# Two open units of VectorE's exponentials with alternating passes, and a normalisation on PE that is held until its input is made

## The chip, the cores and the metric

The kernel runs on one core of one Trainium2 chip. The metric is device time of one execution in microseconds, lower is better. Before the change three runs took 967.95, 971.15 and 971.46 us; the median is 971.15 us.

The engines named here: PE (TensorE, the matmuls; PEld are its weight loads), DVE (VectorE), ACT (ScalarE), POOL (GpSimd) and SP (SyncE, which issues the DMAs).

## The reference

One transformer block on x of shape 1 x 2048 x 640, bf16: layernorm, attention with 32 heads of 20 dimensions over all 2048 positions (no mask), output projection and residual; then layernorm, a gated bilinear layer (gate times up, 1728 wide, no nonlinearity), down projection and residual.

```python
def _A_ref(x, wqkv, wo):
    ...
    q, k, v = qkv[0], qkv[1], qkv[2]
    scores = jnp.einsum("bhqd,bhkd->bhqk", q, k) * (Dh ** -0.5)
    p = _softmax(scores, axis=-1)
    o = jnp.einsum("bhqk,bhkd->bhqd", p, v)
    return (lambda x, *d: x.transpose(*d))(o, 0, 2, 1, 3).reshape(B, S, D) @ wo
def _B_ref(x, w_gate, w_up, w_down):
    g = jnp.einsum("bsd,df->bsf", x, w_gate)
    u = jnp.einsum("bsd,df->bsf", x, w_up)
    h = g * u
    return jnp.einsum("bsf,fd->bsd", h, w_down)
x = A_x
h = x + _A_ref(_layernorm(x, axis=-1), A_wqkv, A_wo)
h2 = h + _B_ref(_layernorm(h, axis=-1), B_w_gate, B_w_up, B_w_down)
```

## The kernel before

The 2048 queries are four blocks of 512 (`QB`), the 32 heads eight groups of four (`HPG`), the 2048 keys sixteen tiles of 128. A *unit* is the 128 x 512 block of scores of one head, one key tile and one query block; 2048 such units are needed. They are laid out one after another into score tiles of 1536 columns (`EW`), three units each, so that there are 683 tiles. Two score tiles fit in PSUM (`scp`), and the exponential of a tile goes to one of six `E` buffers (`ep`).

The units are ordered by *segments* (`segs`): one pass over the keys for one head group and one query block, 64 units or some 21 tiles. Pass 0 does query block 0 (its first four groups by chunks of four key tiles while the keys are still being made), passes 1 and 2 the next two blocks. Of the last block two groups go as pass 3 and the rest as two half blocks of 256 queries, passes A and B.

The whole order of instructions is worked out in Python while the kernel is built: a planner keeps the times at which it thinks that each engine will be free (`at["pe"]`, `at["dve"]`, `at["exp"]` for ScalarE, `at["slot"]` for the score tiles, `at["mi"]` for the one PSUM bank of the side jobs). The main loop takes one tile per round:

- `emit_S` (L440) issues the tile's score matmuls (L450), asks `x_takes` (L474) whether VectorE shall take the last 512 columns, and issues ScalarE's exponential of the rest (L463).
- `emit_AV` (L588) issues up to eight matmuls of the weighted sums (L619) from `av_q`, the queue of finished exponentials; when a segment is complete VectorE copies the sums out of the single `acc` bank into `asb` (L630).
- `run_job` (L429) issues a piece of other matmul work while the next tile's place is not yet free: projections, and behind the attention of each query block the output projection (`out`), the gated layer (`glu`) and its down projection (`y`) of that block. Jobs are generators that yield their PE cost; `step` (L365) takes from `urgent`, then `waiting`, then `jobs`. Where nothing fits, two matmuls keep the PE clock up (`keep_warm`, L427).
- `spare` (L412) issues pending VectorE work where the planner sees VectorE free: layernorm pieces (`aux`) first, then passes of VectorE's exponentials.

**VectorE's exponential** (`emit_x`, L480) is five instructions on 128 x 512: scale and shift out of PSUM (`xv`, L488), bits of the mantissa (`xm`, L498), two polynomial passes (`xt`, L499 and L500), and the sum that is read as bf16 (`xe`, L493). Each reads what the one before it wrote. The first is issued with its tile; the other four go into `x_pieces`, one queue in order, which `step_x` (L513) empties. `x_takes` allows a unit only in segments of kind "only" of passes 0 to 2 (or later, when no job is left), at least three tiles (`X_LEAST`) before the segment's last tile, with fewer than three pieces pending, with VectorE's planned time not over PE's by 200 ns (`TOL`), and with fewer than six (`X_OUT`) units between opening and use. `need_x` (L521) issues all that is pending of a segment before its last weighted sums, and `put_x` (L504) appends finished units to the end of their segment in `av_q`.

**The normalisation** of a segment normally goes over DMAs: sums to DRAM and back into rows, reciprocal, broadcast, multiplication on GpSimd (`norm`, L525). For the three segments of `FAST` (the last group of pass 2, the last of pass A, the last but one of pass B) it is a job on PE instead (`job_norm`, L574): f32 matmuls turn the sums into columns (L559), VectorE takes the reciprocal and spreads it (L563, L565), f32 matmuls turn it back (L571), and VectorE multiplies (L582). It is put into `urgent` as soon as the copy to `asb` has been issued, and `step` takes it at once.

The planner's own numbers: a unit costs VectorE 690 ns for the first pass and 480, 700, 700 and 700 for the others; an exponential costs ScalarE 50 ns and 5/6 ns a column; a switch on PE 110 ns (`SWITCH`), a semaphore 150 ns (`LAT`).

## Time and profile before

| | |
|---|---|
| median of three runs | 971.15 us |
| profiled execution | 968.8 us |
| its span | 966.9 us |
| mean PE clock granted | 0.976 |
| first `xv` (L488) to the last | 141.45 to 684.12 us |
| `xv` instructions | 102 |
| pass L498, mean | 438 ns |
| pass L499, mean | 695 ns |
| passes L500 and L493, mean each | 726 ns |
| keep-warm matmuls (L427) | 189, 61.6 us |
| ScalarE's wait for score tiles (L450), whole span | 22.0 us in 29 waits |
| ScalarE's wait for weighted sums (L619), whole span | 3.5 us in 3 waits |
| PE's wait for ScalarE before score tiles | 55.6 us in 128 waits |

In the lines of a profile, L12 is line 12 of the kernel; `E<-sc` means that E is written from sc; the figures behind the bar are busy microseconds, mean nanoseconds of one, and the time that the engine stood idle just before such instructions, with what ended it. In timeline lines the first two figures are start and duration in microseconds, and the bracket holds the idle time before the instruction and its releaser. Durations on VectorE can overlap: the next instruction may start before the record of the one before it ends. The span leaves out some two microseconds that lie around it in the run's time.

### The profile page before, as it was taken

The page shows a single profiled execution, that of the slowest core. Times are in us where ns is not written, and L with a number is a line of the kernel's source. Part 1 is how long each engine was busy: PE and PEld are TensorE (multiplying, and loading weights), DVE is VectorE, ACT ScalarE, POOL GpSimd, SP SyncE. Part 2 cuts the span into 40 slices and gives each one's busy share as a digit, 9 for nine tenths or more (in the row PEclk, how much of TensorE's full clock was granted, in tenths as well). Part 3 has the DMA queues.
Part 4 walks back from the last instruction along what each step waited for, and adds up shares of the span by engine and source line. Part 5 has one row for each costly group of instructions (what it writes and reads, how often), then busy time and mean ns, then how long its engine had stood idle before and what let it go on. Part 6 is the DMA issues. An engine that isn't in the chain of part 4 may idle for free.

```text
span 966.9 us, 18074 instructions
## 1 busy us (share of the span) xinstructions
PE 837.9 (87%) x7176; PEld 328.5 (34%) x7257; DVE 606.3 (63%) x1224; ACT 899.6 (93%) x719; POOL 61.6 (6%) x155
## 2 busy tenths in 40 slices
PE   7778889888887898998898999988888899888897
PEld 5233333222232222331233223322332334444465
DVE  7664348888778778888878887878462231143243
ACT  6879999999999999999999999999799999899951
POOL 3120011000000000000000000000000000000000
PEclk9999999999999899997999999999799999899999
DMA  6000010010050131014021230103202001102310
GB/s 184 28 1 1 1 26 24 20 39 13 20 178 2 39 85 43 20 43 177 7 68 33 67 87 13 34 20 104 65 3 67 19 8 27 55 19 63 75 42 17
DMA packets 67819, 44.46 MB, mean 46 GB/s; under 512 B 18504, under 2 KB 63404, under 8 KB 67728
## 3 DMA queue, kind: packets, MB, share of 16 engines
q1 hardware_dynamic: 67728, 43.23, 16.0%
q8 instruction: 59, 0.97, 0.4%
q14 instruction: 32, 0.26, 0.1%
HBM read 35.91 MB, written 7.30 MB: 45 GB/s over the span
## 4 chain that ended last, share of the span: by engine, by line
ACT 40%; PE 35%; issue 14%; DVE 9%; DMA 1%; POOL 0%; SPq 0%; ACTq 0%; DVEq 0%; POOLq 0%
ACT E L463 40%; PE sc L450 9%; PE acc L619 6%; PE mi L278 4%; PE mi L900 3%; PE mi L955 3%; PE mi L834 2%; PE f L900 2%; PE mi L427 1%; PE mi L292 1%; PE f L955 1%; DVE kT L285 1%; DVE st L182 1%; PE mi L918 1%; DVE u L247 1%
## 5 line engine op out<-in xcount | busy, mean ns | idle before, releaser
L463 ACT ACTIVATE E<-sc 128x1536 bf16<-128x1536 f32 (+1 forms) x683 | 882.3, 1460 | 27.1 <-PE sc L450 22.0
L450 PE MATMUL sc<-qa,kT 32*128 32x512 bf16 x1536 | 204.6, 390 | 54.2 <-ACT E L463 43.4
L450 PEld LDWEIGHTS <-kT 32*128 32x128 bf16 x2432 | 84.5, 91 | 293.2 <-issue 254.5
L619 PE MATMUL acc<-E,vx 128*32 128x512 bf16 (+1 forms) x2330 | 169.5, 357 | 0.5 <-ACT E L463 0.5
L488 DVE TENSOR_SCALAR xv<-sc 128x512 f32<-128x512 f32 x102 | 70.3, 689 | 38.9 <-PE sc L450 38.2
L278 PE MATMUL mi<-lnT,wp 128*128 128x512 bf16 x284 | 79.5, 380 | 14.0 <-DVE qa L285 6.6
L450 PE MATMUL sc<-qb,kT 32*128 32x256 bf16 (+1 forms) x896 | 69.6, 294 | 14.7 <-ACT E L463 12.3
L549 POOL TENSOR_TENSOR on<-asb,bc 128x512 bf16<-128x512 f32 (+1 forms) x30 | 36.0, 1198 | 718.1 <-DMA bc<-scr 468.7
L500 DVE SCALAR_TENSOR_TENSOR xt<-xt,xm 128x512 f32<-128x512 f32 x102 | 74.0, 726 | 2.3
L493 DVE SCALAR_TENSOR_TENSOR xe<-xt,xv 128x512 int16<-128x512 f32 x102 | 74.0, 726 | 1.3
L499 DVE SCALAR_TENSOR_TENSOR xt<-xm 128x512 f32<-128x512 int32 x102 | 70.9, 695 | 2.2
L619 PEld LDWEIGHTS <-vx 128*32 128x32 bf16 x2432 | 44.4, 96 | 67.4 <-issue 67.2
L955 PE MATMUL mi<-wd,hh 128*128 128x320 bf16 x378 | 66.0, 301 | 0.3 <-DVE xr L959 0.3
L427 PE MATMUL mi<-kT,ident 128*128 128x512 bf16 x189 | 61.6, 397 | 4.0 <-DVE on L582 1.8
L900 PE MATMUL mi<-ln2T,wu 128*128 128x512 bf16 (+1 forms) x158 | 46.0, 387 | 6.0 <-DVE hh L908 5.4
L955 PEld LDWEIGHTS <-hh 128*128 128x128 bf16 x448 | 38.1, 97 | 38.1 <-issue 26.6
L247 DVE CAST u<-mi 128x512 bf16<-128x512 f32 (+1 forms) x42 | 28.9, 688 | 34.9 <-PE mi L900 33.3
L908 DVE TENSOR_TENSOR hh<-mi,u 128x512 bf16<-128x512 f32 (+1 forms) x42 | 28.8, 686 | 33.9 <-PE mi L900 31.3
L900 PE MATMUL mi<-ln2T,wg 128*128 128x512 bf16 (+1 forms) x160 | 44.7, 381 | 5.9 <-DVE u L247 5.3
L498 DVE TENSOR_SCALAR xm<-xv 128x512 int32<-128x512 int32 x102 | 44.7, 438 | 0.5
L278 PEld LDWEIGHTS <-wp 128*128 128x128 bf16 x310 | 25.9, 97 | 55.6 <-issue 39.5
L834 PE MATMUL mi<-wo,on 128*128 128x320 bf16 x224 | 38.4, 303 | 1.5 <-DVE xr L838 1.3
(150 smaller groups left out, 611.3 us busy)
## 6 DMA issues: line engine op xcount, KB each, us to landing
bc<-scr SPq DMA_DIRECT2D x100, 64.0 KB
wu<-in_B_w_up_dram SPq DMA_DIRECT2D x20, 320.0 KB
wg<-in_B_w_gate_dram SPq DMA_DIRECT2D x20, 320.0 KB
qsp<-qa SPq DMA_DIRECT2D x8, 384.0 KB
xr<-in_A_x_dram SPq DMA_DIRECT2D x16, 160.0 KB
out_dram<-xr SPq DMA_DIRECT2D x14, 160.0 KB
wd<-in_B_w_down_dram SPq DMA_DIRECT2D x13, 160.0 KB
xs<-in_A_x_dram SPq DMA_DIRECT2D x3, 640.0 KB
```

The lines of the kernel that those rows point to most:

```text
L278: nc.tensor.matmul(ps[:], lhsT=wslice(m, g, c), rhs=lnT[:, c, ch * QB:(ch + 1) * QB], start=(c == 0), stop=(c == KT - 1))
L427: nc.tensor.matmul(ps[:], lhsT=ident[:], rhs=kT[0][:, 0:BANK], start=True, stop=True)
L450: nc.tensor.matmul(sc[:, o:o + w], lhsT=kT[g][SLOT * j:SLOT * (j + 1), kt * P:(kt + 1) * P], rhs=q_of(g, b, c0, w)[SLOT * j:SLOT * (j + 1) ...
L463: exps = nc.scalar.activation(e[:, 0:n_act], sc[:, 0:n_act], ACT.Exp, bias=EXP_BIAS, scale=SM_SCALE)
L488: took = nc.vector.tensor_scalar(v[:], ps, X_SCALE, X_BASE, ALU.mult, ALU.max)
L493: nc.vector.scalar_tensor_tensor(e[:], t[:], X_C, v[:], ALU.add, ALU.add)
L499: (700, lambda: nc.vector.scalar_tensor_tensor(t[:], m[:], X_A, m[:], ALU.mult, ALU.mult)),
L500: (700, lambda: nc.vector.scalar_tensor_tensor(t[:], t[:], X_B, m[:], ALU.add, ALU.mult)),
L619: nc.tensor.matmul(acc["t"][SLOT * j:SLOT * (j + 1), 0:w], lhsT=vx[kt][:, VS * h:VS * h + SLOT], rhs=e, start=(acc["n"][j] == 0), stop=(ac ...
L834: nc.tensor.matmul(ps[:, 0:HALF], lhsT=on[g][:, t * P:(t + 1) * P], rhs=wo[g][:, cs], start=(g == 0), stop=(g == NG - 1))
L900: nc.tensor.matmul(ps[0:M, 0:n], lhsT=st["w", fp][k][:, c, f2 * P:f2 * P + M], rhs=st["ln2T"][:, c, c0:c0 + n], start=(c == 0), stop=(c == ...
L955: nc.tensor.matmul(ps[:, 0:HALF], lhsT=st["hh"][f][0:K, t * P:(t + 1) * P], rhs=late["Wd"][f][0:K, cs], start=(f == 0), stop=(f == 2 * FP ...
```

## The change

- **Chains.** `x_pieces` becomes `x_chains`, one queue of passes for each open unit, and a unit may be opened while one other is open (`len(x_chains) < 2`, where it was fewer than three pending pieces). `next_x` picks the first chain other than the one whose pass was issued last on VectorE; a chain's last pass is not taken ahead of an older chain. Any other VectorE work in between clears that memory (`x_prev`). `step_x` charges 90 ns less (`X_DEP`) for a pass that does not follow its own chain.
- **Limits.** With more than two passes pending a unit must lie six tiles ahead of its segment's last tile, otherwise three as before. `X_OUT` is five instead of six, and live units are a queue that is emptied in order, so that a unit counts until it and all older ones are used. `xm` and `xt` have two buffers.
- **Normalisation on PE.** `opens` holds the planned time at which `asb` is ready, and `first` keeps the job in `urgent` until then, unless there is nothing else to do. `job_norm` now tells the planner its PE and VectorE costs and is two pieces instead of three; `sums_to_rows` is split so that its matmuls come from `sums_on_pe`.
- **Weighted sums.** `emit_AV` looks at the oldest exponential in the queue, where it looked at the first, and goes on although the `acc` bank isn't planned free when the oldest is `E_BUFS` (six, as before) rounds old; the main loop calls it a second time in a round when the oldest is five rounds old or more.

```diff
--- before.py
+++ after.py
@@ -55,7 +55,8 @@
 EXP_NS, EXP_END, EXP_COL = 50, 166, 5 / 6
 S_NS, S_EXP, SWITCH, LAT = 323, 500, 110, 150
 TOL, LEAST, MARGIN = 200, 430, 100
-X_LEAST, X_OUT = 3, 6
+X_LEAST, X_OUT, X_DEP = 3, 5, 90
+E_BUFS = 6
 SHIFT = 1184.0
 LOG2E = 1.4426950408889634
 X_UNIT = 128.0
@@ -93,7 +94,7 @@
     qkp = pool("qkp")
     vp = pool("vp")
     onp = pool("onp")
-    ep = pool("ep", 6)
+    ep = pool("ep", E_BUFS)
     nrm = pool("nrm", 2)
     xp = pool("xp")
     small = pool("small", 2)
@@ -229,6 +230,7 @@
     def dve(ns):
         ready = at["pe"] + LAT
         spare(ready)
+        x_prev["chain"] = None
         at["dve"] = max(at["dve"], ready) + ns
 
     def apply1(t, m32, r, k, eng=None):
@@ -326,11 +328,12 @@
         tiles.append((cur_t, pos))
 
     last_tile = {s: i for i, (us, _) in enumerate(tiles) for s, *_ in us}
-    x_pieces = deque()
+    x_chains = deque()
+    x_prev = {"chain": None}
     x_left = {}
     x_put = []
-    x_live = {"units": 0}
-    x_last = set()
+    x_live = deque()
+    x_used = set()
 
     av_q = deque()
     acc = {"seg": None, "t": None, "from": 0, "left": 0}
@@ -339,6 +342,7 @@
     jobs = deque()
     urgent = deque()
     waiting = deque()
+    opens = {}
     aux = deque()
     events = []
     cur = {"key": None, "gen": None, "fresh": True}
@@ -362,11 +366,14 @@
             events.remove(ev)
             ev[1]()
 
+    def first():
+        return urgent and (opens.get(urgent[0][0], 0) < at["pe"] + SWITCH or not (waiting or jobs or cur["gen"]))
+
     def step():
-        if cur["fresh"] and (urgent or waiting):
+        if cur["fresh"] and (first() or waiting):
             if cur["gen"] is not None:
                 jobs.appendleft((cur["key"], cur["gen"]))
-            cur["key"], cur["gen"] = (urgent or waiting).popleft()
+            cur["key"], cur["gen"] = (urgent if first() else waiting).popleft()
         c = advance()
         if c == WAIT:
             waiting.append((cur["key"], cur["gen"]))
@@ -404,13 +411,14 @@
         while aux:
             try:
                 at["dve"] += next(aux[0]) or 200
+                x_prev["chain"] = None
                 return True
             except StopIteration:
                 aux.popleft()
         return False
 
     def spare(until):
-        while at["dve"] + (x_pieces[0][0] if x_pieces and not aux else 600) <= until + TOL:
+        while at["dve"] + (next_x()[0][0] if x_chains and not aux else 600) <= until + TOL:
             if not step_aux() and not step_x():
                 break
 
@@ -419,7 +427,7 @@
             if not step_aux():
                 raise RuntimeError(f"nothing makes {key}")
 
-    COST = {"T": 300, "v": 680}
+    COST = {"T": 300, "v": 680, "nf": 780}
 
     def keep_warm():
         ps = bank()
@@ -428,8 +436,9 @@
 
     def run_job(until):
         if cur["fresh"]:
-            key = urgent[0][0] if urgent else cur["key"] if cur["gen"] is not None else jobs[0][0] if jobs else None
-            if not waiting and (key is None or max(at["pe"], at["mi"]) + SWITCH + COST.get(key[0], LEAST) > until):
+            key = urgent[0][0] if first() else cur["key"] if cur["gen"] is not None else jobs[0][0] if jobs else None
+            begin = max(at["pe"], at["mi"], opens.get(key, 0))
+            if not waiting and (key is None or begin + SWITCH + COST.get(key[0], LEAST) > until):
                 return key is not None
         begun = at["pe"]
         while at["pe"] + 216 <= until + 60:
@@ -474,31 +483,31 @@
     def x_takes(i):
         us, n = tiles[i]
         s = us[-1][0]
-        return (n == EW and segs[s][4] == "only" and (PASS[segs[s][0]][0] < LAST_B or not jobs and not cur["gen"]) and last_tile[s] - i >= X_LEAST and len({u[0] for u in us}) == 1
-                and len(x_pieces) < 3 and at["dve"] < at["pe"] + TOL and x_live["units"] < X_OUT)
+        return (n == EW and segs[s][4] == "only" and (PASS[segs[s][0]][0] < LAST_B or not jobs and not cur["gen"]) and last_tile[s] - i >= X_LEAST + (3 if sum(map(len, x_chains)) > 2 else 0) and len({u[0] for u in us}) == 1
+                and len(x_chains) < 2 and at["dve"] < at["pe"] + TOL and len(x_live) < X_OUT)
 
     def emit_x(ps, us):
         s = us[0][0]
         w = PASS[segs[s][0]][2]
         v = xp.tile([P, BANK], F32, name="xv", bufs=2)
-        m = xp.tile([P, BANK], I32, name="xm")
-        t = xp.tile([P, BANK], F32, name="xt")
+        m = xp.tile([P, BANK], I32, name="xm", bufs=2)
+        t = xp.tile([P, BANK], F32, name="xt", bufs=2)
         e = xp.tile([P, BANK], I16, name="xe", bufs=X_OUT)
         dve(690)
         took = nc.vector.tensor_scalar(v[:], ps, X_SCALE, X_BASE, ALU.mult, ALU.max)
-        x_live["units"] += 1
+        x_live.append((s, us[-1][1], us[-1][2]))
         x_left[s] = x_left.get(s, 0) + 1
 
         def last():
             nc.vector.scalar_tensor_tensor(e[:], t[:], X_C, v[:], ALU.add, ALU.add)
             x_left[s] -= 1
             x_put.append([(now["i"], s, kt, j, e[:, o:o + w].bitcast(BF16)) for s, kt, j, o in us])
-            x_last.update({(s, us[-1][1], us[-1][2])})
-        x_pieces.extend([
+        x_chains.append(deque([
             (480, lambda: nc.vector.tensor_scalar(m[:], v[:].bitcast(I32), 0x7FFF, 0x8000, ALU.bitwise_and, ALU.bitwise_or)),
             (700, lambda: nc.vector.scalar_tensor_tensor(t[:], m[:], X_A, m[:], ALU.mult, ALU.mult)),
             (700, lambda: nc.vector.scalar_tensor_tensor(t[:], t[:], X_B, m[:], ALU.add, ALU.mult)),
-            (700, last)])
+            (700, last)]))
+        x_prev["chain"] = x_chains[-1]
         return took
 
     def put_x():
@@ -510,11 +519,19 @@
                 av_q.insert(k, u)
         x_put.clear()
 
+    def next_x():
+        chain = next((c for c in x_chains if c is not x_prev["chain"]), x_chains[0])
+        return x_chains[0] if len(chain) == 1 else chain
+
     def step_x():
-        if not x_pieces:
+        if not x_chains:
             return False
-        ns, fn = x_pieces.popleft()
-        at["dve"] += ns
+        chain = next_x()
+        ns, fn = chain.popleft()
+        at["dve"] += ns - (X_DEP if chain is not x_prev["chain"] else 0)
+        x_prev["chain"] = chain
+        if not chain:
+            x_chains.remove(chain)
         fn()
         return True
 
@@ -551,12 +568,14 @@
             later(8, mult)
         later(5, back)
 
-    def sums_to_rows(asb, w):
-
-        n = w // SLOT
+    def sums_on_pe(asb, w):
         ps = bank()
         for t in range(w // P):
             nc.tensor.matmul(ps[:, HPG * t:HPG * (t + 1)], lhsT=asb[:, t * P:(t + 1) * P], rhs=identf[:, DH:P:SLOT], start=True, stop=True)
+        return ps
+
+    def sums_to_rows(ps, w):
+        n = w // SLOT
         r16 = sums_all[:, col["n"]:col["n"] + n]
         col["n"] += n
         ri = nrm.tile([P, n], F32, name="ri", tag=f"ri{n}")
@@ -574,10 +593,14 @@
     def job_norm(s, asb):
         p, g = segs[s][0:2]
         b, c0, w = PASS[p]
-        bc = sums_to_rows(asb, w)
-        yield NEXT
+        ps = sums_on_pe(asb, w)
+        yield 780 * w // QB
+        dve(700)
+        bc = sums_to_rows(ps, w)
         yield NEXT
         ps = rows_to_cols(bc, w, bank())
+        yield 1030 * w // QB
+        dve(690 * w // QB)
         assert b == 0 or ("om", b - 1) in done
         nc.vector.tensor_tensor(On[g][:, c0:c0 + w], asb[:, 0:w], ps[:, 0:w], ALU.mult)
         done.add(("n", p, g))
@@ -592,11 +615,11 @@
         if acc["seg"] is not None and av_q[0][1] != acc["seg"]:
             need_x(acc["seg"])
             put_x()
-        i, s = av_q[0][0:2]
+        s = av_q[0][1]
         p, g, lo, hi, kind = segs[s]
         b, c0, w = PASS[p]
         if acc["seg"] != s:
-            if at["pe"] < at["acc"] and now["i"] < acc["from"]:
+            if at["pe"] < at["acc"] and now["i"] < acc["from"] and min(u[0] for u in av_q) > now["i"] - E_BUFS:
                 return
             acc["seg"], acc["left"], acc["n"] = s, (hi - lo) * HPG, [0] * HPG
             acc["t"] = accp.tile([P, QB], F32, name="acc")
@@ -607,13 +630,14 @@
             if len(rows[u[3]]) < most // HPG:
                 rows[u[3]].append(u)
         ready = sum(len(r) for r in rows)
-        if ready < min(most, acc["left"]) and i > upto - 3:
+        if ready < min(most, acc["left"]) and min(u[0] for u in av_q) > upto - 3:
             return
         for u in [r[k] for k in range(most // HPG) for r in rows if k < len(r)]:
             av_q.remove(u)
             _, _, kt, j, e = u
-            if (s, kt, j) in x_last:
-                x_live["units"] -= 1
+            x_used.add((s, kt, j))
+            while x_live and x_live[0] in x_used:
+                x_live.popleft()
             ensure(("v", kt, g // (NG // 2)))
             h = HPG * g + j
             nc.tensor.matmul(
@@ -637,6 +661,7 @@
             if s == FINAL:
                 final["asb"] = asb
             elif (p, g) in FAST:
+                opens["nf", p, g] = at["dve"] + LAT
                 urgent.append((("nf", p, g), job_norm(s, asb)))
             elif kind in ("only", "last"):
                 norm(s, asb)
@@ -1052,7 +1077,7 @@
                                  rhs=wo[NG - 1][:, hf * HALF:(hf + 1) * HALF], start=False, stop=True)
         ta, tb = LAST_T
         out_most(ta, 0)
-        bc = sums_to_rows(asb, HW)
+        bc = sums_to_rows(sums_on_pe(asb, HW), HW)
         out_most(ta, 1)
         ps = rows_to_cols(bc, HW, accp.tile([P, QB], F32, name="acc"))
         for k in range(2):
@@ -1136,7 +1161,10 @@
         if i == n_tiles:
             root = small.tile([P, 1], BF16, name="root")
             nc.scalar.activation(root[:], ones[:], ACT.Sqrt)
-        emit_AV(i if i >= n_tiles else i - 2 if i >= LAG else i - 4)
+        for _ in range(2):
+            emit_AV(i if i >= n_tiles else i - 2 if i >= LAG else i - 4)
+            if not av_q or min(u[0] for u in av_q) > i - E_BUFS + 1:
+                break
         run_events(i)
         if b_seen < NB - 1 and normed(str(b_seen), range(NG)):
             add_tail(b_seen, list(range(TPB)))
```

## The prediction

> **What bounds the kernel now.** I read the page's busy lines first, then the groups, then the windows of the middle stretch, and last the timeline where ScalarE stood still.
>
> ```profile
> span 966.9 us, 18074 instructions
> ...
> PE 837.9 (87%) x7176; PEld 328.5 (34%) x7257; DVE 606.3 (63%) x1224; ACT 899.6 (93%) x719; POOL 61.6 (6%) x155
> ...
> DVE  7664348888778778888878887878462231143243
> ACT  6879999999999999999999999999799999899951
> ```
>
> ScalarE (ACT) is at 9 in nearly every slice, VectorE (DVE) at 7 to 8 up to about slice 28 and far lower after it. The windows view of 140 to 684 us, where VectorE takes its share of the exponentials, and the groups of L463 with shapes kept apart say what a unit is worth:
>
> ```profile
> 140.00:684.00 544.00, 479.91 (x3596) 157.11 (x3643) 435.55 (x795) 537.11 (x430) 31.29 (x22) 0.98 0.18 52
> ```
>
> ```profile
> L463 ACT ACTIVATE E<-sc 128x1536 bf16<-128x1536 f32 x580 | 803.5, 1524 | 24.4 <-PE sc L450 19.6 <-PE acc L619 3.5
> L463 ACT ACTIVATE E<-sc 128x1024 bf16<-128x1024 f32 x103 | 113.6, 1103 | 2.8 <-PE sc L450 2.4
> ```
>
> The columns of the first are PE, PEld, DVE, ACT and POOL busy, then the clock. ScalarE is busy 537.1 of 544 us: it is the bound, and 430 tiles pass there. A tile of which VectorE takes 512 columns costs ScalarE 1103 instead of 1524 ns, so **one unit more is worth 421 ns** as long as the others keep up. VectorE opened 102 units (L488) and is not busy for 544.0 - 435.6 = 108.4 us here. PE has 544 - 479.9 = 64 us not busy, and the window's group of L427, matmuls that only keep it warm, holds another 49.4.
>
> **Part 1, two open units with alternating passes.** Removed: nothing that runs; a unit is still five instructions. Moved: the order of its four later passes. Added: as many units as the planner finds room for. First what alternation saves, from VectorE's timeline (start, duration):
>
> ```profile
> 306.14 0.68 DVE L500 SCALAR_TENSOR_TENSOR xt<-xt,xm 128x512 f32<-128x512 f32 x1
> 306.85 0.69 DVE L493 SCALAR_TENSOR_TENSOR xe<-xt,xv 128x512 int16<-128x512 f32 x1
> 307.46 0.42 DVE L498 TENSOR_SCALAR xm<-xv 128x512 int32<-128x512 int32 x1
> 307.92 0.69 DVE L499 SCALAR_TENSOR_TENSOR xt<-xm 128x512 f32<-128x512 int32 x1
> 308.64 0.69 DVE L500 SCALAR_TENSOR_TENSOR xt<-xt,xm 128x512 f32<-128x512 f32 x1
> 309.37 0.69 DVE L493 SCALAR_TENSOR_TENSOR xe<-xt,xv 128x512 int16<-128x512 f32 x1
> 309.98 0.48 DVE L247 COPY ln2T<-mi 128x640 bf16<-128x640 bf16 x1
> ```
>
> Start to start, a pass that reads what the one before wrote comes after 0.71, 0.72 and 0.73 us; one that does not comes after 0.61 us (306.85 to 307.46, and 309.37 to 309.98), before the earlier record has ended. So a broken pair is worth about 0.11 us, and the planner's new X_DEP of 90 ns is on the safe side. The Trainium skill ("VectorE: DVE Perf Modes", section "The DRAIN you can't avoid") speaks against it: the next operation starts only once the pipe is empty, whatever is chained. By it alternation would save nothing on the engine; the 0.61 beside 0.72 differs, so I keep the rows.
>
> The planner charges a unit 690 + 480 + 3 x 700 = 3270 ns today, in whatever company its passes run; after the change 2910 when none of the four follows its own unit. With nine passes in ten so placed (my choice: two chains are open most of the time, and other work breaks pairs too) it is 3270 - 0.9 x 360 = 2946. Two estimates of the number of units: (a) the same planned VectorE time holds 102 x 3270 / 2946 = 113, so 11 more. (b) Of the 101 distances between openings, counted in score tiles, 33 are exactly three tiles and eight shorter. A run of such starts shows why:
>
> ```profile
> 656.21 0.69 DVE L488 TENSOR_SCALAR xv<-sc 128x512 f32<-128x512 f32 x1 [1.76 <-PE sc L450]
> ...
> 659.81 0.69 DVE L488 TENSOR_SCALAR xv<-sc 128x512 f32<-128x512 f32 x1 [0.53 <-PE sc L450]
> ...
> 663.41 0.69 DVE L488 TENSOR_SCALAR xv<-sc 128x512 f32<-128x512 f32 x1 [0.53 <-PE sc L450]
> ```
>
> 3.60 us for three tiles, with 0.53 us of it idle: the rule that a new unit needs fewer than three pending passes rounds up to whole tiles. Two units in five tiles take 5 x 1.33 - 2 x 0.43 = 5.8 us of planned ScalarE time and 2 x 2.91 = 5.8 of planned VectorE, so 2.5 tiles a unit just goes: 99 tiles would hold 40 units instead of 33, 7 more, and the other 60 or so distances at (a)'s eleven per cent give 7. That is 14. I take **14 more units**, 14 x 0.421 = 5.9 us. Bounds: none more (six tiles before a segment's end instead of three when over two passes are pending, and at most five live units counted in order; below none by perhaps 4, if the count of five binds), and 30 more (30 x 2.79 us real, the sum of 0.61 x 4 and 0.35, is 84 of the 108 free): -2 to 13 us. What else they cost: PE has the room named above. Each new L488 and its passes stand in VectorE's queue in front of an evacuation; PE waited 1.2 us in the window for L488, and 6.9 + 6.5 for the two evacuations of L900 over the span. More passes may add a fifth of that; with PE's reserve I take 1.5 us lost, between 0 and 4.
>
> **Part 2, the last normalisation of a block.** Three jobs take this way. At the end of pass 2:
>
> ```profile
> 685.46 1.56 PE L559 MATMUL mi<-identf,asb 128*128 128x4 f32 x8 [1.09 <-DVE asb L630]
> ...
> 687.67 2.79 ACT L463 ACTIVATE E<-sc 128x1536 bf16<-128x1536 f32 x2 [1.81 <-PE sc L450]
> ...
> 688.01 2.05 PE L571 MATMUL mi<-identf,bc 128*128 128x128 f32 x8
> ...
> 692.50 1.45 ACT L463 ACTIVATE E<-sc 128x1536 bf16<-128x1536 f32 x1 [2.03 <-PE sc L450]
> ...
> 694.98 5.48 ACT L463 ACTIVATE E<-sc 128x1536 bf16<-128x1536 f32 x4 [1.03 <-PE sc L450]
> ```
>
> PE stands 1.09 us on the copy of the sums, and the next score tiles are behind it; then the 2.05 us of L571 run between tiles with nothing charged for them. ScalarE loses 1.81 + 2.03 + 1.03 = 4.9 us. At the end of pass A the same pattern costs 0.38 + 1.78 + 0.47 + 0.22 = 2.85 us (837 to 846 us), at the last one 0.56: 8.3 in all. The change holds the job back until the copy is planned done, so the 1.09, 0.59 and 0.27 us that PE waits go; it charges 780 and 1030 ns where the trace has 1.56 and 2.05, so half the rest stays. The wait is the planner's, not a semaphore; behind it in the urgent queue stand only the later load and out jobs, and ordinary jobs run instead. No DMA moves. I take **3.5 us gained**, between 8 and a loss of 1 (the out-projection of that block starts later).
>
> **Part 3, the weighted sums.** They go by the oldest exponential in the queue and may be issued twice in a round. ScalarE waited 3.5 us for L619 (the form row above), 1.53 of it at 312.88, followed by 0.99 and 0.92 for late score tiles. I take 1 us gained, between 3.4 and a loss of 2 (smaller groups, one more switch each). Two extra xm and xt buffers and one xe fewer cost no time.
>
> Sum: 5.9 - 1.5 + 3.5 + 1 = 8.9 us. Against the profiled run, 968.8 us with its 966.9 of span, that is 959.9. The three runs are 967.95, 971.15 and 971.46, so the profiled one lies 2.35 under their median; the same sum from the median gives 962.3. I forecast **962 us**.
>
> **The rivals.**
> 1. *The new units don't come.* The limit of five live units, popped in order, or the distance to the segment's end refuses what the second chain would open. For: a unit at 480.21 is used by L619 only at 490.24 us, some eight tiles later, so at one per 2.5 tiles over three are alive, more in bursts. Against: that is under five. Then parts 2 and 3 and little else: 971.15 - 3 = 968.
> 2. *Slower: the end of a segment.* The new order finishes two units late together; the last weighted sum of the segment, the single acc bank and the six E buffers behind it wait for both. For: at 309.37 it happened with one unit (L619 waited 1.01 us for xe), and ScalarE lost 1.53 + 0.99 + 0.92 = 3.4 us. Against: a second unit is opened only up to six tiles, 7.6 us, before the segment's last when more than two passes are pending, and eight passes at 0.61 us are under 5. It outweighs the 8.9 us from the third segment of 24 on; with five it is 17 us less 8.9: 979.
> 3. *Nothing saved by alternation.* By the rule above the planner would count 0.36 us a unit that VectorE doesn't have, 115 x 0.36 = 41 us late over the stretch, out of the 108 free; half of it hits evacuations and the gain of part 1 is gone: 969. The rows make this unlikely.
> 4. *More room than I count*, 25 to 30 units and most of the norms' waits: 971.15 - 12 - 6 = 953.
>
> **The numbers.** Under 0.5% (4.9 us) is what I count as no change. Forecast 0.54 (958 to 966.2), rival 1 0.16, rival 2 0.16, rival 3 0.03, rival 4 0.11. Faster: 0.54 + 0.11 + a little of rival 1, 0.67. Same: 0.17, the rest of rivals 1 and 3. Slower: 0.16. The range reaches from rival 4's time to a weak form of rival 2: 953 to 973.
>
> **What would show it.** Right: about 116 instructions at L488 and as many more exponentials of 1024 columns; distances of two tiles mixed with three; passes of two units in turn at 0.61 us; L559 no longer waiting for asb; ScalarE's gaps at the end of passes 2 and A about half. Wrong: L488 near 102, or ScalarE's wait for L450 and L619 between 140 and 684 us rising from its 6.9 us in the window to 12 or more.

## The result and the profile after

The changed kernel takes 982.59 us (median of four runs, 979.30 to 984.52) against 969.61 us for the kernel before (967.95 to 971.46): ratio 1.0139, 95% interval 1.0109 to 1.0168. It is slower by 1.4%, where 962 us had been forecast.

The page of the changed kernel (busy lines, and two of the slice rows):

```profile
span 980.1 us, 18165 instructions
...
PE 854.0 (87%) x7223; PEld 328.5 (34%) x7223; DVE 616.2 (63%) x1259; ACT 898.9 (92%) x719; POOL 61.6 (6%) x155
...
DVE  7664448878878788777878787787562331242232
ACT  6879999989999999899999999999999999997941
```

ScalarE's forms of L472 (L463 before), shapes apart:

```profile
L472 ACT ACTIVATE E<-sc 128x1536 bf16<-128x1536 f32 x573 | 792.4, 1508 | 29.2 <-PE sc L459 21.2 <-PE acc L643 6.0
L472 ACT ACTIVATE E<-sc 128x1024 bf16<-128x1024 f32 x110 | 117.5, 1094 | 10.4 <-PE sc L459 7.2 <-PE acc L643 2.8
```

VectorE takes seven units more (109 for 102), and ScalarE's busy time is the same within 1 us (898.9 for 899.6). The span grew by 13.2 us, so the loss is ScalarE standing idle. The wait view of 140 to 700 us says for what (in total, times, longest), the changed kernel first, then the one before:

```profile
ACT E L472 <- PE sc L459: 9.2, 17, 1.5
ACT E L472 <- PE acc L643: 7.1, 4, 3.0
```

```profile
ACT E L463 <- PE sc L450: 9.1, 14, 2.0
ACT E L463 <- PE acc L619: 1.7, 2, 1.5
```

The 9.1 of before include 4.9 for the normalisation at the end of pass 2, of which 0.8 is left, at 700 us. Where the time went is read best by comparing when each segment's sums are copied to `asb` (one VectorE instruction a segment, in the same order in both). The difference of the two profiled runs, after less before:

| stretch (time before, us) | it changes by | and stands at |
|---|---|---|
| to 143 | +1.0 | +1.0 |
| 143 to 339 (at +8.3 at 311) | +3.4 | +4.4 |
| 339 to 658 | +8.1 | +12.5 |
| 658 to 853, the normalisations of pass 2 and A | -7.8 | +4.7 |
| 853 to 883 | +4.2 | +8.9 |
| 883 to 926 | +1.8 | +10.7 |
| 926 to the end | +2.5 | +13.2 |

So there is one gain, as forecast, and there are losses in three places, each of which has its own cause below: up to 339 us, from 339 to 658, and from 853 to 883.

### The profile page after: what moved, and what is told of

Its sections match the earlier page's. It is cut to its first block, busy times and chain, and to the rows that moved or that the text cites. A ratio compares the mean times of both kernels' runs of the same rounds, so it can differ in the third digit from the quotient of the medians.

```text
span 980.1 us, 18165 instructions
## 1 busy us (share of the span) xinstructions
PE 854.0 (87%) x7223; PEld 328.5 (34%) x7223; DVE 616.2 (63%) x1259; ACT 898.9 (92%) x719; POOL 61.6 (6%) x155
## 4 chain that ended last, share of the span: by engine, by line
ACT 39%; PE 31%; issue 15%; DVE 12%; DMA 2%; POOL 1%; SPq 0%; ACTq 0%; DVEq 0%; POOLq 0%
ACT E L472 39%; PE sc L459 7%; PE acc L643 5%; PE mi L925 3%; PE mi L280 3%; PE mi L980 3%; PE mi L435 2%; PE mi L943 2%; PE f L925 2%; DVE xe L502 1%; DVE st L183 1%; PE mi L294 1%; PE f L980 1%; DVE xm L506 1%; DVE qa L287 1%
## 5 line engine op out<-in xcount | busy, mean ns | idle before, releaser
L472 ACT ACTIVATE E<-sc 128x1536 bf16<-128x1536 f32 (+1 forms) x683 | 881.4, 1441 | 39.7 <-PE sc L459 28.4
L643 PE MATMUL acc<-E,vx 128*32 128x512 bf16 (+1 forms) x2322 | 172.4, 359 | 4.0 <-DVE asb L654 3.9
L497 DVE TENSOR_SCALAR xv<-sc 128x512 f32<-128x512 f32 x109 | 74.8, 687 | 44.2 <-PE sc L459 43.1
L280 PE MATMUL mi<-lnT,wp 128*128 128x512 bf16 x310 | 87.1, 392 | 15.6 <-DVE qa L287 8.4
L502 DVE SCALAR_TENSOR_TENSOR xe<-xt,xv 128x512 int16<-128x512 f32 x109 | 77.8, 715 | 0.8
L507 DVE SCALAR_TENSOR_TENSOR xt<-xm 128x512 f32<-128x512 int32 x109 | 76.8, 709 | 0.6
L435 PE MATMUL mi<-kT,ident 128*128 128x512 bf16 x182 | 57.7, 400 | 0.6 <-DVE ln2T L249 0.3
L925 PE MATMUL mi<-ln2T,wg 128*128 128x512 bf16 (+1 forms) x170 | 46.7, 381 | 9.0 <-DVE u L249 9.0
L925 PE MATMUL mi<-ln2T,wu 128*128 128x512 bf16 (+1 forms) x170 | 48.2, 386 | 4.1 <-DVE hh L933 4.1
L506 DVE TENSOR_SCALAR xm<-xv 128x512 int32<-128x512 int32 x109 | 49.8, 461 | 0.5
```

Of the source, the lines that this page charges most:

```text
L280: nc.tensor.matmul(ps[:], lhsT=wslice(m, g, c), rhs=lnT[:, c, ch * QB:(ch + 1) * QB], start=(c == 0), stop=(c == KT - 1))
L435: nc.tensor.matmul(ps[:], lhsT=ident[:], rhs=kT[0][:, 0:BANK], start=True, stop=True)
L472: exps = nc.scalar.activation(e[:, 0:n_act], sc[:, 0:n_act], ACT.Exp, bias=EXP_BIAS, scale=SM_SCALE)
L497: took = nc.vector.tensor_scalar(v[:], ps, X_SCALE, X_BASE, ALU.mult, ALU.max)
L502: nc.vector.scalar_tensor_tensor(e[:], t[:], X_C, v[:], ALU.add, ALU.add)
L506: (480, lambda: nc.vector.tensor_scalar(m[:], v[:].bitcast(I32), 0x7FFF, 0x8000, ALU.bitwise_and, ALU.bitwise_or)),
```

## The experiments

Times are medians beside runs of the kernel before on the same chip, whose medians lay between 967.45 and 968.65 us; the ratio is to those.

**The parts alone.** Three parts can be put on the kernel before or taken from the changed one: the normalisation on PE, the weighted-sum rules, and the two open units, which are run here only together with the sum rules. (The reason is argued and no run shows it: without those rules a weighted sum that would free an E buffer comes to stand behind work that waits for that buffer.)

```diff
 p_units: the changed kernel, with
-            key = urgent[0][0] if first() else cur["key"] if ...
+            key = urgent[0][0] if urgent else cur["key"] if ...
...
 p_norm: before, with first(), opens, sums_on_pe and the costs in job_norm
 p_sums: before, with the three rules of emit_AV and the main loop
 p_norm_sums: both
```

> The changed kernel with the normalisation on PE as it was before (two open units and the new weighted-sum rules stay; two open units alone aren't possible without those rules). Theory U (the two open units lose the time, at the ends of segments): slower than before by 15 to 20 us, since the 5 us that the normalisation gave at the ends of passes 2 and A are lost too, so 985 to 990. Theory W (the weighted-sum rules lose it): the same here; the run of those rules alone tells. Theory N (the normalisation's planning loses it late, at 880 us and in the last 50 us): about 975.

> The kernel before with only the normalisation's wait and costs. Theories U and W: faster than before by 4 to 7 us, 963 to 966, the gaps at the ends of passes 2 and A being gone. Theory N: 972 or more, with ScalarE standing still 3 us or more for a late weight load near 880 us.

> The kernel before with only the weighted-sum rules (oldest exponential, two calls in a round). Theory U: within 2 us of before. Theory W: slower by 8 us or more, 978.

> Everything but the two open units. Theory U: 963 to 966, as the normalisation alone, so the two open units cost 17 to 20 us in the changed kernel. Theory W: 975 or more. Theory N: 975 or more with the loss after 850 us.

| run | us | ratio, 95% interval | units |
|---|---|---|---|
| p_units | 977.93 | 1.0090 (1.0057 to 1.0124) | 108 |
| p_norm | 961.13 | 0.9920 (0.9890 to 0.9949) | 102 |
| p_sums | 974.94 | 1.0068 (1.0043 to 1.0093) | 101 |
| p_norm_sums | 968.46 | 0.9998 (0.9976 to 1.0019) | 101 |

The normalisation alone gains 7.4 us, the sum rules alone lose 6.4, and together they cancel. None of the three theories fits all four runs. N falls with p_norm, which was to be at 972 or more. W has the sign right in p_sums, but p_norm_sums was to be at 975 or more. U expected 963 to 966 there and 985 to 990 for p_units. The units on top of the sum rules cost 3 us without the normalisation, which lies within the intervals of the two runs, but 14 with it (982.6 against 968.5). So the parts don't add up: what one of them costs depends on the order of work that the others leave.

**Which sum rule, and the order of the passes.**

```diff
 q_oldest
-        if ready < min(most, acc["left"]) and i > upto - 3:
+        if ready < min(most, acc["left"]) and min(u[0] for u in av_q) > upto - 3:
 q_acc
-            if at["pe"] < at["acc"] and now["i"] < acc["from"]:
+            if at["pe"] < at["acc"] and now["i"] < acc["from"] and min(u[0] for u in av_q) > now["i"] - E_BUFS:
 q_two
-        emit_AV(i if i >= n_tiles else i - 2 if i >= LAG else i - 4)
+        for _ in range(2):
+            emit_AV(i if i >= n_tiles else i - 2 if i >= LAG else i - 4)
+            if not av_q or min(u[0] for u in av_q) > i - E_BUFS + 1:
+                break
 q_in_order: p_units, with
-        return x_chains[0] if len(chain) == 1 else chain
+        return x_chains[0]
```

> The kernel before with one of the three weighted-sum rules: a group of weighted sums goes when the oldest exponential of the queue is due, not the first one. Theory F (the rule issues small groups early, which break up the order that was worked out): 4 to 7 us slower, 973 to 976. Theory G (the acc bank's rule is it): within 1.5 us of before. Theory H (two calls in a round are it): within 1.5 us of before.

> The kernel before with one of the three weighted-sum rules: a new segment's weighted sums are issued although the acc bank isn't planned free, when an exponential is six rounds old. Theory G: PE stands about 1 us on the copy of the last segment's sums in several segments, with the score matmuls behind it; 4 to 7 us slower. Theories F and H: within 1.5 us of before.

> The kernel before with one of the three weighted-sum rules: a second call in a round when an exponential is five rounds old. Theory H: two groups of eight weighted sums (1.0 to 1.3 us) stand between two score tiles, ScalarE waits for the second, and 4 to 7 us are lost. Theories F and G: within 1.5 us of before.

> The changed kernel without its normalisation part, and with two units open but their passes one unit after the other. Theory E (alternation finishes both units late, and the segment's last sums wait): ScalarE's 7.1 us of waits for the weighted sums between 140 and 700 us fall to 3 to 4 as in the run of the sum rules alone, and the time is 4 us under the 977.9 of the run with alternation. Theory K (any more units on VectorE than before do it): the waits stay at 6 or more and the time is 976 to 980.

| run | us | ratio, 95% interval |
|---|---|---|
| q_oldest | 977.89 | 1.0104 (1.0074 to 1.0133) |
| q_acc | 967.98 | 0.9998 (0.9983 to 1.0014) |
| q_two | 969.14 | 1.0005 (0.9987 to 1.0022) |
| q_in_order | 971.21 | 1.0032 (1.0015 to 1.0049) |

Of the three rules only the oldest-exponential one costs anything, 9.2 us; that is theory F's rule, but the next set shows another reason for about half of it. With the passes in order the wait for the weighted sums falls from 7.1 us in p_units to 1.3, and the time by 6.7 us (5.6 by the ratios), more than theory E expected and not as theory K did.

**A queue.** In the changed kernel's SP queue (issue time and duration), the sums of the segment that ends at 203 us stand behind 32 loads of `wo`:

```profile
194.96 11.92 SPq L805 DMA_DIRECT2D wo<-in_A_wo_dram  x32
206.98 0.51 SPq L549 DMA_DIRECT2D sums<-asb  x1
208.69 0.35 SPq L550 DMA_DIRECT2D sums_all<-sums  x1
211.65 0.35 SPq L557 DMA_DIRECT2D scr<-ri  x1
```

Its VectorE timeline has the reader of those sums, and its ScalarE timeline what follows:

```profile
211.37 0.25 DVE L555 RECIPROCAL ri<-sums_all 128x16 f32<-128x16 f32 x1 [2.38 <-DMA sums_all<-sums]
```

```profile
213.27 2.44 ACT L472 ACTIVATE E<-sc 128x1024 bf16<-128x1024 f32 x2 [1.48 <-PE sc L459]
216.20 1.45 ACT L472 ACTIVATE E<-sc 128x1536 bf16<-128x1536 f32 x1 [0.49 <-PE sc L459]
218.23 3.71 ACT L472 ACTIVATE E<-sc 128x1024 bf16<-128x1024 f32 x3 [0.58 <-PE sc L459]
```

The reciprocal (L538 before) is put into VectorE's queue five rounds after the copy. It stood 2.38 us there; behind it is the copy of a projection out of the one `mi` bank, behind that PE's next job, and behind that the score tiles:

```profile
211.54 0.67 DVE L287 TENSOR_SCALAR qa<-mi,shift_row 128x512 bf16<-128x512 f32 x1
212.26 0.59 PE L280 MATMUL mi<-lnT,wp 128*128 128x512 bf16 x2 [2.43 <-DVE qa L287]
212.78 0.39 PE L459 MATMUL sc<-qa,kT 32*128 32x512 bf16 x3
```

Before, the loads went out from 189.84 us and the same wait was 0.90 us; in q_oldest it was 3.4, in p_sums 3.2, in p_norm_sums 4.3.

```profile
205.20 0.25 DVE L538 RECIPROCAL ri<-sums_all 128x16 f32<-128x16 f32 x1 [0.90 <-DMA sums_all<-sums]
```

```diff
 r_wo_queue: the changed kernel, r_oldest_wo: q_oldest, with
-                nc.sync.dma_start(wo[g][SLOT * j:SLOT * j + DH, :], ...
+                nc.gpsimd.dma_start(wo[g][SLOT * j:SLOT * j + DH, :], ...
 r_in_order: the changed kernel with the edit of q_in_order
 r_old_limit: the changed kernel, with
-                and len(x_chains) < 2 and at["dve"] < at["pe"] + TOL and len(x_live) < X_OUT)
+                and sum(map(len, x_chains)) < 3 and at["dve"] < at["pe"] + TOL and len(x_live) < X_OUT)
```

> The whole changed kernel, but the passes of two open units run one unit after the other. Theory E (alternation finishes two units late at a segment's end): ScalarE's waits for the weighted sums between 140 and 700 us fall from 7.1 to under 2.5, and the time from 982.6 to 962 to 968. Theory K (it is the number of units): 978 or more, since the planner still opens 106.

> The whole changed kernel, passes alternate, but a new unit still needs fewer than three pending passes. Theory E: the waits for the weighted sums stay at 5 or more and the time at 977 or more, since two units still finish together. Theory L (the looser rule for opening loses it, not the order of the passes): 970 or less.

> The whole changed kernel with the 32 loads of wo issued by GpSimd's queue instead of SP's; every instruction of PE and VectorE stays in its place. Theory Q (VectorE's reciprocal near 211 us stands 2.4 us for sums whose DMA is behind those loads in SP's queue, and what is behind it on VectorE holds PE and ScalarE): that wait goes, the segment that ends near 231 us is done 2 to 3 us earlier, and the time falls by 2 to 4 us. Its rival: the loss there is the weighted sums' own, and the time stays within 1 us.

> The kernel before with the oldest-exponential rule alone, and the loads of wo on GpSimd's queue. Theory Q: of the 9.2 us that this rule costs, 3.5 to 5 come from the 3.4 us wait of the reciprocal near 212 us, so 972.5 to 974.5. Rival: it stays at 977 to 979.

| run | us | ratio, 95% interval | ScalarE's wait for sums, 140 to 700 us |
|---|---|---|---|
| r_wo_queue | 972.16 | 1.0069 (1.0046 to 1.0092) | 7.1 |
| r_oldest_wo | 972.33 | 1.0054 (1.0035 to 1.0073) | 4.3 |
| r_in_order | 970.91 | 1.0029 (1.0011 to 1.0048) | 1.6 |
| r_old_limit | 969.14 | 1.0019 (0.9996 to 1.0042) | 2.3 |

In r_wo_queue every instruction of PE and VectorE stays in its place, and the SP queue is free for the sums:

```profile
201.24 0.50 SPq L549 DMA_DIRECT2D sums<-asb  x1
203.03 0.34 SPq L550 DMA_DIRECT2D sums_all<-sums  x1
206.64 0.34 SPq L557 DMA_DIRECT2D scr<-ri  x1
```

The reciprocal starts without a wait:

```profile
206.37 0.25 DVE L555 RECIPROCAL ri<-sums_all 128x16 f32<-128x16 f32 x1
```

How much that is worth is not read well from the medians. They differ by 10.4 us, but they come from different sets of runs, and the nine runs of r_wo_queue fall into two groups, 971.4 to 972.2 and 976.0 to 978.1. By the ratios it is 6.8 us, and the intervals leave room for 3 to 10. The copies to `asb` of the two profiled runs say where: they are 2.5 us apart already at 171 us, before any load of `wo` goes out, 5.7 at the copy that stands at 226 us before, and 6.4 at 339. PE and VectorE have the same order in both, so the first 2.5 us are run-to-run difference, and **3 to 4 us come at the place itself**. For q_oldest and r_oldest_wo the same three figures are 3.3, 7.7 and 7.2, which makes about 4 us (4.8 by the ratios, 5.6 by the medians). Theory Q holds, at about the size that was expected. What is left of the cost of the oldest-exponential rule, 0.54% in r_oldest_wo, stays open; theory F's small groups are neither shown nor ruled out for it.

Theory E as put falls: with alternation but the old limit the time is 969.1 and the waits 2.3, where 977 and 5 were expected. It takes both, the alternation and a unit opened while more than two passes are pending. These two runs can't price it, though. Their order of work near 211 us is another too, and the reciprocal's longest wait for its sums is 0.8 us in r_in_order and 0.7 in r_old_limit, so they lose the queue's cost as well. And r_in_order stays above the 962 to 968 that were expected; it still loses 4.2 us between 853 and 883 us, as the changed kernel does. The run t_far_end below starts from r_wo_queue and separates the causes.

**The end of a segment, and another queue.** What both together do is seen in the changed kernel's VectorE timeline before its longest wait:

```profile
315.92 0.42 DVE L506 TENSOR_SCALAR xm<-xv 128x512 int32<-128x512 int32 x1
316.26 0.68 DVE L508 SCALAR_TENSOR_TENSOR xt<-xt,xm 128x512 f32<-128x512 f32 x1
316.86 0.68 DVE L507 SCALAR_TENSOR_TENSOR xt<-xm 128x512 f32<-128x512 int32 x1
317.46 0.68 DVE L502 SCALAR_TENSOR_TENSOR xe<-xt,xv 128x512 int16<-128x512 f32 x1
318.89 0.69 DVE L654 COPY asb<-acc 128x512 f32<-128x512 f32 x1 [0.75 <-PE acc L643]
319.50 0.68 DVE L508 SCALAR_TENSOR_TENSOR xt<-xt,xm 128x512 f32<-128x512 f32 x1
```

```profile
320.34 5.05 ACT L472 ACTIVATE E<-sc 128x1536 bf16<-128x1536 f32 x4 [3.01 <-PE acc L643]
```

Passes of the other unit stand between those of the unit that this segment still needs; its xe ends near 318.1, the sums are copied at 318.89, the next segment's sums can't start before that, its exponentials fill the six E buffers, and ScalarE stands 3.01 us for a free one. The unit that the segment needs had been opened at 293.40 us already; its second pass comes at 312.70, since layernorm pieces, which go first, hold VectorE from 305.99 to 312.10. The other was opened at 313.04 and belongs to the next segment, as it is finished only behind the copy of the sums.

Late in the kernel, the SP queue again. First the kernel before, where a pair of weight loads goes out ahead of `scr` and `bc`, then the changed one:

```profile
869.30 0.47 SPq L880 DMA_DIRECT2D wu<-in_B_w_up_dram  x1
869.87 0.48 SPq L880 DMA_DIRECT2D wg<-in_B_w_gate_dram  x1
874.56 0.34 SPq L540 DMA_DIRECT2D scr<-ri  x1
876.79 1.72 SPq L543 DMA_DIRECT2D bc<-scr  x4
```

```profile
877.18 0.34 SPq L557 DMA_DIRECT2D scr<-ri  x1
878.66 2.53 SPq L560 DMA_DIRECT2D bc<-scr  x4
881.29 0.39 SPq L905 DMA_DIRECT2D wu<-in_B_w_up_dram  x1
```

```profile
884.78 0.72 PE L943 MATMUL mi<-ln2T,wu 128*128 128x256 bf16 x5 [3.13 <-DMA wu<-in_B_w_up_dram]
```

```profile
886.62 2.98 ACT L472 ACTIVATE E<-sc 128x1536 bf16<-128x1536 f32 x2 [3.68 <-PE sc L459]
```

```diff
 t_far_end: r_wo_queue, with
-    last_tile[s] - i >= X_LEAST + (3 if sum(map(len, x_chains)) > 2 else 0)
+    last_tile[s] - i >= X_LEAST + (8 if sum(map(len, x_chains)) > 2 else 0)
 t_weights_queue: r_wo_queue, with
-        nc.sync.dma_start(view[:, :, 0:w], src[...])
+        nc.gpsimd.dma_start(view[:, :, 0:w], src[...])
 t_norm_wo: p_norm with the edit of r_wo_queue
 t_alt_queues: r_old_limit with both queue edits
 u_all_three: r_wo_queue with both edits, far end and weights
```

> The changed kernel with the wo loads on GpSimd's queue (972.2 us in that form), and with a second busy unit opened only eleven tiles before its segment's last instead of six; the planner opens 108 units where it opened 109. Theory S (two units that alternate and were opened with more than two passes pending end late at the segment's end, and hold the acc bank and the E buffers): ScalarE's 7.1 us of waits for the weighted sums fall under 3.5, the stretch of the segments that end between 339 and 658 us loses under 4 us against before instead of 10, and the time is 965 to 968. Rival M (any such order disturbs the plan, wherever in the segment): the waits stay at 5 or more and the time at 970 to 975.

> The changed kernel with the loads of wo and of the gate and up weights on GpSimd's queue; PE, VectorE and ScalarE keep their order. Theory Q2 (PE's 2.8 to 3.1 us wait for a weight tile near 884 us comes from SP's queue, where the load stands behind the four broadcasts of a normalisation): that wait goes under 1 us and the time falls from 972.2 to 967 to 969. Rival: the load waits for its buffer, not for the queue; the wait stays and the time is within 1.5 us of 972.2.

> The kernel before with the normalisation part alone, and the loads of wo on GpSimd's queue. The reciprocal's wait of 1.0 us near 205 us goes; 960 to 961 against the 961.1 without it, as the wait was mostly hidden there. Theory Q holds if it isn't slower.

> The changed kernel with the old limit for opening a unit (969.1 us in that form) and with the loads of wo, gate and up on GpSimd's queue. Theories S and Q2 together: the wait for weights near 884 us goes and 4 to 6 us with it, 963 to 965. If alternation with 107 units is worth anything beyond the normalisation alone it is under 961.

> The changed kernel with all three losses taken away: wo, gate and up loads on GpSimd's queue, and a second busy unit only eleven tiles or more before its segment's last. If the three are the whole loss and add up: 982.6 - 10.4 - 4.8 - 3.8 = 963.6, so 962 to 965, the wait for weights near 884 us gone and the waits for the weighted sums under 2. If something else is left: 967 or more.

| run | us | ratio, 95% interval |
|---|---|---|
| t_far_end | 967.33 | 0.9982 (0.9965 to 1.0000) |
| t_weights_queue | 968.33 | 1.0001 (0.9985 to 1.0018) |
| t_norm_wo | 961.76 | 0.9931 (0.9906 to 0.9956) |
| t_alt_queues | 962.46 | 0.9945 (0.9927 to 0.9963) |
| u_all_three | 960.86 | 0.9933 (0.9912 to 0.9954) |

ScalarE's waits in t_far_end, 140 to 700 us:

```profile
ACT E L472 <- PE sc L459: 5.3, 12, 1.7
ACT E L472 <- PE acc L643: 1.3, 1, 1.3
```

The 7.1 us are 1.3, with 108 units: of the 3.01 us near 320 us 1.3 are left, and the three other waits, 1.8, 1.3 and 1.0 us, are gone. Between the segments that end at 339 and 658 us it loses 1.4 us against before, where the changed kernel lost 8.1 and r_wo_queue 10.1. So 8.7 us come at this place (8.4 by the ratios, 4.8 by the medians), with one unit fewer. Theory S holds, and theory K (the number of units) is out. In t_weights_queue the load goes out earlier, from GpSimd's queue, as soon as its buffer is free, and no wait of PE for weights is left there in its wait view. From 853 to 883 us it gains 1.3 us against before, where r_wo_queue loses 3.7, so 5.0 us come at this place (6.6 by the ratios, 3.8 by the medians). Q2 holds:

```profile
875.04 0.90 POOL L905 DMA_DIRECT2D wu<-in_B_w_up_dram  x1 [5.22 <-PE mi L943]
```

The three together were expected at 963.6 as a sum of medians and came to 960.86, a little under the range of 962 to 965. By the ratios the sum is 1.0139 less 0.0070, 0.0087 and 0.0068, which is 0.9914 and lies within the interval of the measured 0.9933. So the three mechanisms account for the loss against the kernel before. The run t_alt_queues came between its two expectations, 963 to 965 and under 961, and decides nothing.

No gain of the units is seen: the changed kernel without its losses has 108 units and is no faster than p_norm with 102 (ratios 0.9933 and 0.9920, intervals overlapping). That is not their price, since the first also has the sum rules, whose remaining cost is open. Both, like t_norm_wo and t_alt_queues, beat the kernel before and the changed one; p_norm is the smallest edit among them, and its loads need no other queue (t_norm_wo gains nothing).

## Why the prediction was wrong

- **The bound** was read rightly: ScalarE, at 421 ns a unit.
- **The broken pair** of passes, 0.11 us, is there. In the changed kernel, with units in turn:

```profile
577.86 0.68 DVE L933 TENSOR_TENSOR hh<-mi,u 128x512 bf16<-128x512 f32 x1
578.46 0.68 DVE L508 SCALAR_TENSOR_TENSOR xt<-xt,xm 128x512 f32<-128x512 f32 x1
579.05 0.42 DVE L506 TENSOR_SCALAR xm<-xv 128x512 int32<-128x512 int32 x1
579.39 0.68 DVE L502 SCALAR_TENSOR_TENSOR xe<-xt,xv 128x512 int16<-128x512 f32 x1
579.99 0.68 DVE L507 SCALAR_TENSOR_TENSOR xt<-xm 128x512 f32<-128x512 int32 x1
```

  0.60, 0.59, 0.34 and 0.60 us from start to start. The rule of the Trainium skill, "VectorE: DVE Perf Modes", section "The DRAIN you can't avoid", by which the next operation waits until the pipe is empty, doesn't hold for these instructions as the prediction put it; the section itself adds that a next operation that isn't held starts earlier, and these rows agree with that. Rival 3 is out. Of the four later passes of a unit, 55% followed something other than their own unit's pass in the kernel before and 82% do in the changed one, where nine in ten had been taken.
- **The units**: 14 were taken and 7 came, at 421 ns each 2.9 us for 5.9, of which ScalarE's busy time shows 0.7. Estimate (a), with 11, was nearer than (b). Which limit held them to seven isn't shown. The distance to the segment's end alone doesn't explain it: with eleven tiles instead of six only one unit fewer is opened.
- **The normalisation**: 3.5 us were taken, 7.4 measured alone, near the upper bound of 8. The term is too small by its own working: 1.95 us of PE's waits and half of the other 6.35 us of gaps make 5.1. I had left that half in place because the planned costs are under the measured ones; p_norm's profile has 4.2 us of waits for score tiles between 140 and 700 us for 9.1 before, and none between 840 and 900.
- **The weighted sums**: a gain of 1 us was taken, with a loss of at most 2. Alone they lose 6.4. This is the term with the wrong sign. Only the oldest-exponential rule costs anything, and about half of what it costs is the next point.
- **The step that failed** is the sentence "No DMA moves". No DMA was added, but the whole order is worked out anew, so each DMA came to stand elsewhere in SP's queue against the others. I had priced the change on PE, VectorE and ScalarE only, and never asked what stands behind what in the queue that all loads share. Twice something short and urgent (a segment's sums, a weight tile) came behind something long or waiting, which cost 3 to 4 us near 211 us and 5.0 near 884.
- **The second step that failed**, and the larger one, is the argument against rival 2: a second unit is opened six tiles, 7.6 us, before the segment's last, and eight passes at 0.61 us are under 5. That leaves out VectorE's other work, the 6 us of layernorm pieces near 309 us above all, and passes of a unit of the next segment, at which the rule on the distance doesn't look. Six tiles are not enough; with eleven the loss is gone but for 1.4 us (8.7 us less). Rival 2 named this mechanism with its place and got a chance of 0.16; the rows at 309.37 us that spoke for it should have weighed more than an estimate of room. That its 979 us came near the measured time is luck: it priced this loss alone at 17 us, twice of what it is, and had neither of the two queues. The prediction's own sign of being wrong came: ScalarE stood idle before exponentials for 17.8 us between 140 and 684 us, where 12 had been named and 6.9 was the time before.

## What to carry to other kernels

Where the order of all work comes out of a planner, a change to one rule moves everything: list for each in-order queue, the DMA-issuing one included, which short transfers someone waits for and what may come to stand ahead of them, and price that before the gain. A consumer put into an engine's queue a fixed number of rounds after its DMA is only as safe as the DMA queue is empty; a plan-neutral experiment, the same instructions with the loads on another queue, shows it in one run. Its size is read at the place, against a marker ahead of it: here two runs with the same order stood 2.5 us apart before the edit had issued anything. And interleaving two chains shortens their sum but lengthens each, which costs where something waits for a particular one: here near the end of a segment.

## What the runs showed that had not been expected

The granted PE clock falls where PE is starved, and the matmuls behind a stall are slower: six score matmuls take 0.61 us at 890 us in the changed kernel and 0.40 at 894. The windows of the changed kernel (the column behind the busy times is the clock):

```profile
210.00:220.00 10.00, 7.04 (x42) 1.76 (x41) 7.10 (x11) 7.46 (x7) 1.49 (x1) 0.83 0.10 28
220.00:230.00 10.00, 9.22 (x70) 2.84 (x67) 7.55 (x13) 9.88 (x9) 0.00 (x0) 1.00 0.00 0
310.00:320.00 10.00, 6.36 (x50) 2.11 (x51) 8.21 (x21) 7.33 (x6) 0.00 (x0) 0.81 0.00 1
880.00:890.00 10.00, 6.13 (x60) 3.18 (x57) 1.70 (x4) 5.84 (x5) 0.72 (x1) 0.81 0.27 76
890.00:900.00 10.00, 9.77 (x127) 5.28 (x128) 3.11 (x9) 8.41 (x7) 0.00 (x0) 0.85 0.02 3
```

PE is busy 6 to 7 of 10 us in the three stalls and the clock is 0.81 to 0.83; after the last one it is still 0.85 while PE is busy 9.77. The kernel before has such a place too: its clock is 0.50 from 313 to 320 us of its own time, behind the 1.01 us that PE stood for `xe` at 309. The Trainium skill, "TensorE: Matmul & The Clock Gate", section "Part 1: The HAM clock gate", has the clock halve after about 3.4 us of idle PE. The direction agrees. The length doesn't: PE's longest idle time in these stalls is 2.43 us near 211 us, 0.85 near 316 and 3.13 near 884, and in the kernel before, where the clock is 0.56 already from 310 to 313 us, none between 295 and 313 is longer than 1.01. In the last 55 us the changed kernel's clock is 0.89 where it was 0.99 before, 2.5 us of the span. The change of order alone doesn't cause that: with the same order on PE and VectorE the clock there is 0.96 in r_wo_queue and 0.98 in t_weights_queue. Chance there is: of twelve runs of r_in_order, the same instructions each time, the one with a mean clock of 0.965 took 976.52 us and the one with 0.980 took 966.34.
